# A fused linear-attention and gated-FFN kernel: one list of steps exchanged for another

## The chip, the cores and the metric

The kernel runs on one core of one Trainium2 chip. The metric is the device time of that core in microseconds (us), the median of the runs shown. Five engines work side by side: TensorE (PE in the profile, with PEld for its weight loads), VectorE (DVE), ScalarE (ACT), GpSimd (POOL) and SyncE (SP). Here POOL and SP do almost nothing but issue DMAs. Each engine takes its instructions strictly in program order; semaphores hold an instruction until what it reads has been written.

## The reference

Eight batches, eight heads, 576 positions, head size 64. Per batch and head a 64x64 matrix `kv` is made from k and v, q is multiplied by it, and each row of the product is normalised. The heads are laid side by side (512 columns) and go through a feed-forward part with a gate made by a convolution over three positions.

```python
kv = np.einsum('bhsd,bhse->bhde', k, v)
out = np.einsum('bhsd,bhde->bhse', q, kv)
rms = np.sqrt(np.mean(out * out, axis=-1, keepdims=True) + 1e-06)
attn = out / rms * g_norm                       # -> x: (8, 576, 512)
h = np.maximum(x @ w_in, 0.0)                   # (8, 576, 1024)
for k in range(3):
    conv_out += conv_w[k][None, None, :] * hp[:, k:k + S, :]
gate = 1.0 / (1.0 + np.exp(-conv_out))
result = h * gate @ w_out                       # (8, 576, 512)
```

Inputs and output are 32-bit floats. Inside, the operands of the matrix products are bf16.

## The kernel before

The whole program is unrolled from one string, `ORDER` (line 67). Each word of it is a step: `name.arguments:choice@slots`. A loop (line 802) calls the function of that name; what the function issues goes to the end of the queue of the engine that does it. After the loop every instruction is tied behind the one before it on its engine, so `ORDER` fixes the order on all five engines at once, the order of the DMA issues included. There is no scheduler behind it. The `choice` says which of two engines does a copy or a relu; the `slots` say which PSUM bank (0 to 7) or which buffer of a small ring a step writes, and a step waits until the last readers of that slot are done.

The steps, in the order in which a batch b passes them (t is one of four pairs of heads, f one of eight blocks of 128 columns of h, j a pair of such blocks, e a half of the positions):

- `Lq`, `Lk`, `Lv` (line 304) load q, k or v of a batch from memory, 576 KB in bf16, from POOL's queue; `Li` and `Lo` load a quarter of w_in and a half of w_out the same way. Batch 0 comes in smaller pieces and batch 1 in halves (288 KB). q, k and v have two buffers each (`@0`, `@1`), so a load waits until the batch that was in its buffer has been used.
- `kv.b.0.4` multiplies k by v for all head pairs (line 361, 48 products of one batch). `kvc`, or `kvn` with `ky` or `kx`, copy the result to SBUF: `kvn` straight, `ky` a half of it crossed over by an engine, `kx` the same by a DMA from SP's queue.
- q is transposed: by PE (`qt`, `qtp`) and a copy (`qc`) in batches 0 to 4, by a transposing DMA from SP's queue (`dq.b.0`, `dq.b.1`, line 439) in batches 5, 6 and 7.
- `ot` or `oq` multiplies q by kv, `sq` squares it on ACT, `oc` copies it to SBUF; `on` or `ss` sums the squares on PE, `nl` or `ln` takes the reciprocal root on ACT; `mu0` or `mu` multiplies into x on DVE. From batch 2 on the factors are spread over the positions by PE (`sl`, `sp`), for batches 6 and 7 through memory (`fw`, `fr`).
- `hm.b.f` is the product x times w_in (line 643), for the first blocks split into `ha` and `hb`; `re` is the relu, on ACT (line 649) or DVE (line 651).
- `ta`, `aa`, `ab` make the convolution on DVE, `sg` the sigmoid on ACT, `mg` the product with h on DVE. Sigmoid and reciprocal root need different tables, so ACT reloads a table at each change.
- `om.p.m` is the product with w_out for 128 positions of a pair p of batches (line 764), in one go or in two halves; `ea` copies it out of PSUM, `st` stores it from SP's queue. The last tile is split (`oh`, `eh`, `sh`).
- `unread` issues matrix products that nobody reads; `pl` fills a small mask on POOL; `al` takes a buffer for x or h.

The batches are taken in the order 0, 1, 2, 3, 4, 5, 7, 6 up to the normalisation. While PE makes h of one batch, DVE and ACT work on the gate of the one before, and loads run one to two batches ahead. In the list before, the loads of the last two batches stand in this order, with their buffers:

```python
Lq.7.0@0 Lv.7.0@0 Lk.7.0@0 Lv.6.0@1 Lk.6.0@1 Lq.6.0@1
```

Of the kernel before, what the change touches and what calls it, by code (L numbers as in the profile page):

```python
# [67 lines left out]
pre@0,0,0 Lq.1.0@1 unread.10.0@1 qt0.0.0@0 qt0.0.1@1 ca.k.0:1 pi ca.v.0:1 qc0.0.0:1@0 unread.2.2@2  # L68
kv.0.0.1@3 pn kv.0.1.1@2 kvc.0.0.1.0:1@0 kvc.0.0.1.1 kvc.0.1.1.1 qc0.0.1 unread.3.4@0 kvc.0.1.1.0 ot.0.1@4 ct@1
unread.1.3@0 sq.0.1@0 pg Li.1 unread.2.1@2 on.0.1@0 ot.0.0@6 qt0.0.2@2 pc Li.3 nl.0.1@0 Lk.1.0@1 sq.0.0@0 al.x0@0  # L70
kv.0.2.1@3 kvc.0.2.1.0:1 kvc.0.2.1.1:1 unread.1.1@0 Lv.1.0@1 Li.0 mu0.0.1 on.0.0@0 qc0.0.2:1@0 nl.0.0@1 Lk.1.2 al.h0@0
qt0.0.3@3 ot.0.2@4 sq.0.2@0 kv.0.3.1@2,0 mu0.0.0 qc0.0.3:1 on.0.2@6 unread.3.2@1 kvc.0.3.1.0 kvc.0.3.1.1:1 nl.0.2@0
# [15 lines left out]
qc.4.0:1@0 hm.2.4@0 om.0.2.4 re.2.4 sg.1.6 sg.1.1 sp.3.1@6,3 sg.1.0 ea.0.0:1@2 mu.3.1.1 mu.3.1.0 Lq.5.0@1 hm.2.2@0
aa.1.2 kv.4.0.4@5 re.2.2 ea.0.2@3 Lv.5.0@1 kvn.4.0.4 sp.3.0@6,3 mu.3.0.1 hm.2.5@0 sg.1.3 mu.3.0.0 ab.1.2 hm.2.7@2
re.2.5 dq.5.0@2 re.2.7 hm.3.5@6 mg.1.0 mg.1.3 hm.3.4@0 ky.4.0.4.0 Lk.5.0@1 sg.1.2 hm.2.6@2 ky.4.0.4.1:1 oq.4.0@4  # L90
re.3.4:1 oq.4.1@0 sg.1.5 ta.2.4@0 re.3.5 dq.5.1@1 re.2.6 ta.2.5 sq.4.0@0 oc.4.0@0 hm.3.1@6 re.3.1 mg.1.1 hm.3.3@2
aa.2.2 qtp.4.1@4 sq.4.1@1 qc.4.1@0 hm.3.6@6 oc.4.1 sg.1.4 mg.1.2 om.0.8.0@0 oq.4.2@4 re.3.3 oq.4.3@2 Lq.7.0@0 re.3.6
# [758 lines left out]
```

## Time and profile before

| what | us |
|---|---|
| time, median of three runs | 176.12 (176.03 to 178.52) |
| span of the profiled execution, first to last instruction | 174.7 |
| PE busy | 164.6 |
| DVE busy | 151.8 |
| ACT busy | 144.0 |
| POOL busy | 30.8 |

The profile is of one execution; it gives its span, and the time of that execution beyond the span is not given with it. Between the span and the median of the three runs lie 1.4 us.

Besides the page, four kinds of answers of the trace are used below. A table by windows gives for each stretch of the span its length and, per engine, the busy time and the number of instructions, then PE's granted clock, the DMA share and the bytes moved. A timeline row is start, duration, engine, line, operation, out<-in, shape and count, with the idle time before it in brackets and what ended it; a `q` behind the engine's name means its sequencer, which issues a DMA. A group row has busy time and mean duration of one behind the bar. A DMA row is out<-in, the issuing queue, count, KB, and the us from issue to landing.

### The profile page before, as it was taken

To read this page: it belongs to the slowest core of one execution; us is meant where nothing else is said; L and a number is where in the kernel's file an instruction comes from. 1 tells how busy PE (TensorE), PEld (TensorE's weight loads), DVE (VectorE), ACT (ScalarE), POOL (GpSimd) and SP (SyncE) were. 2 spreads that over 40 slices of the span, in tenths; PEclk is the share of its full clock that TensorE was granted. 3 is DMA by queue.
4 is the path that set the end of the run, shared out by engine and by line. 5 is a ranking of instruction groups with operands and counts; after the bars stand their busy time and mean duration, and the time that the engine had idled before them with its cause. 6 is when DMAs were issued, how large, how long until landed. Compare 5 with 4: busy or idle time off the path is not lost.

```text
span 174.7 us, 3978 instructions
## 1 busy us (share of the span) xinstructions
PE 164.6 (94%) x1590; PEld 100.1 (57%) x1607; DVE 151.8 (87%) x248; ACT 144.0 (82%) x224; POOL 30.8 (18%) x54
## 2 busy tenths in 40 slices
PE   6988997899799999999999999999999999999992
PEld 2545765685644687744677774545687654444451
DVE  4166799999999999999999999999989999998520
ACT  4578897999999999999999998999988629766132
POOL 7994705313130001810000000000000000000000
PEclk9999999999999999999999999999999999999999
DMA  5999999999999999999999390477694400076285
GB/s 151 182 186 198 200 202 203 205 204 204 208 203 205 203 204 164 162 196 191 190 203 234 72 261 6 149 188 181 173 268 161 152 0 4 23 277 235 90 322 196
DMA packets 37450, 30.81 MB, mean 176 GB/s; under 512 B 8608, under 2 KB 32952, under 8 KB 37432
## 3 DMA queue, kind: packets, MB, share of 16 engines
q0 software_dynamic: 21760, 15.96, 60.7%
q1 hardware_dynamic: 15632, 14.59, 29.6%
q8 instruction: 12, 0.20, 0.4%
q14 instruction: 6, 0.05, 0.1%
q10 hardware_dynamic: 40, 0.01, 0.0%
HBM read 34.88 MB, written 9.73 MB: 255 GB/s over the span
## 4 chain that ended last, share of the span: by engine, by line
PE 76%; DVE 9%; DMA 4%; POOL 4%; ACT 2%; issue 2%; POOLq 0%; ACTq 0%
PE bank L764 35%; PE bank L643 30%; DMA w_in_sb<-in_moe_w_in_dram 4%; PE bank L361 3%; PE bank L467 2%; DVE taps L703 1%; DVE qT L346 1%; POOL q_sb L245 1%; DVE taps L709 1%; DVE h L754 1%; PE bank L606 1%; DVE taps L702 1%; POOL v_sb L245 1%; POOL k_sb L245 1%; PE bank L781 1%
## 5 line engine op out<-in xcount | busy, mean ns | idle before, releaser
L643 PE MATMUL bank<-xT,w_in_sb 128*128 128x288 bf16 x480 | 63.6, 286 | 0.3 <-ACT root L545 0.2
L764 PE MATMUL bank<-w_out_sb,h 128*128 128x512 bf16 x267 | 62.4, 379 | 0.8 <-issue 0.3
L643 PEld LDWEIGHTS <-w_in_sb 128*128 128x128 bf16 x480 | 46.0, 98 | 14.9 <-issue 1.6
L748 ACT ACTIVATE taps<-taps,cwn 128x1152 bf16<-128x1152 bf16 (+1 forms) x38 | 39.7, 1078 | 7.4 <-DVE taps L715 7.3
L764 PEld LDWEIGHTS <-h 128*128 128x128 bf16 x280 | 26.4, 98 | 31.0 <-issue 1.2
L649 ACT ACTIVATE h<-bank 128x576 bf16<-128x576 f32 x48 | 30.2, 656 | 3.0 <-PE bank L643 2.8
L344 ACT ACTIVATE row<-bank 128x512 f32<-128x512 f32 (+1 forms) x29 | 16.3, 595 | 8.8 <-PE bank L764 6.0
L754 DVE TENSOR_TENSOR h<-h,taps 128x2304 bf16<-128x2304 bf16 (+1 forms) x20 | 22.0, 1109 | 0.6 <-ACT taps L748 0.6
L709 DVE TENSOR_TENSOR taps<-taps 128x2304 bf16<-128x2304 bf16 (+1 forms) x19 | 21.5, 1134 | 0.2
L715 DVE TENSOR_TENSOR taps<-taps,h 128x2304 bf16<-128x2304 bf16 (+1 forms) x19 | 21.5, 1131 | 0.2
L496 ACT ACTIVATE sq<-bank 128x576 bf16<-128x576 f32 x28 | 17.8, 663 | 0.6 <-PE bank L467 0.3
L703 DVE TENSOR_SCALAR taps<-h,cwn 128x1152 bf16<-128x1152 bf16 (+1 forms) x38 | 17.8, 467 | 0.0
L702 DVE TENSOR_SCALAR taps<-h,cwn 128x1152 bf16<-128x1152 bf16 (+1 forms) x38 | 17.4, 457 | 0.3 <-ACT h L649 0.2
L217 ACT ACT_TABLE_LOAD x12 | 15.4, 1283 | 2.6 <-issue 2.4
L651 DVE TENSOR_SCALAR h<-bank 128x576 bf16<-128x576 f32 x16 | 11.8, 752 | 1.7 <-PE bank L643 0.8
L344 ACT ACTIVATE o<-bank 128x576 f32<-128x576 f32 x19 | 12.8, 674 | 0.0
L632 DVE SCALAR_TENSOR_TENSOR xT<-o,cw,bank 128x576 bf16<-128x576 f32 x16 | 12.2, 808 | 0.1
L304 POOL DMA_DIRECT2D q_sb<-in_q_dram x8 | 6.2, 770 | 30.2 <-PE bank L391 29.4
L430 PE MATMUL bank<-fill 128*128 128x512 bf16 x25 | 9.0, 481 | 1.5 <-DVE fill L232 1.5
L346 DVE COPY row<-bank 128x512 f32<-128x512 f32 (+1 forms) x8 | 5.4, 672 | 4.4 <-PE bank L781 2.4
L361 PE MATMUL bank<-v_sb,k_sb 96*64 96x64 bf16 x384 | 8.3, 197 | 0.7 <-ACT sq L496 0.5
L361 PEld LDWEIGHTS <-k_sb 96*64 96x64 bf16 x384 | 7.1, 112 | 2.9 <-issue 2.2
(94 smaller groups left out, 148.8 us busy)
## 6 DMA issues: line engine op xcount, KB each, us to landing
out_dram<-row SPq DMA_DIRECT2D x35, 256.0 KB, 2.6
q_sb<-in_q_dram POOLq DMA_DIRECT2D x6, 576.0 KB, 15.2
v_sb<-in_v_dram POOLq DMA_DIRECT2D x6, 576.0 KB, 14.6
k_sb<-in_k_dram POOLq DMA_DIRECT2D x6, 576.0 KB, 16.6
factor<-factor SPq DMA_DIRECT2D x8, 288.0 KB, 5.4
w_in_sb<-in_moe_w_in_dram POOLq DMA_DIRECT2D x4, 256.0 KB, 9.0
w_out_sb<-in_moe_w_out_dram POOLq DMA_DIRECT2D x2, 512.0 KB, 18.3
q_sb<-in_q_dram POOLq DMA_DIRECT2D x4, 144.0 KB, 4.7
```

Of the source, the lines that this page charges most:

```text
L344: nc.scalar.activation(to, fr, AX.Copy)
L361: nc.tensor.matmul(ps[i][i * D:(i + 1) * D, t - t0, :], k_sb[:, 2 * t + i, r * D:(r + 1) * D], v_sb[:, 2 * t + i, r * D:(r + 1) * D], star ...
L496: nc.scalar.activation(in_order(b, s), product(b, t), AX.Square)
L643: nc.tensor.matmul(ps[:, e, :HS], w_in_sb[:, t, f * P:(f + 1) * P], x[:, t, e * HS:(e + 1) * HS], start=(t == 0), stop=(t == NT - 1))
L649: nc.scalar.activation(to, fr, AX.Relu)
L702: nc.vector.tensor_scalar_mul(tap[:, 0, f % 2, :n, 8:8 + S], h[:, f], cwn[:, 0, f:f + 1])
L703: nc.vector.tensor_scalar_mul(tap[:, 1, f % 2, :n, :S], h[:, f], cwn[:, 2, f:f + 1])
L709: nc.vector.tensor_add(tap[:, 1, :, :n, :S], tap[:, 0, :, :n, 7:7 + S], tap[:, 1, :, :n, 1:1 + S])
L715: nc.vector.tensor_add(y, y, h[:, 2 * j:2 * j + 2])
L748: nc.scalar.activation(y, y, AX.Sigmoid, scale=cwn[:, 1, f:f + 1])
L754: nc.vector.tensor_mul(h, h, T["tap", c, j][:, 1, :, :n, :S])
L764: nc.tensor.matmul(T["om", p, m], h[:, f, m * P:(m + 1) * P], w_out_sb[:, f, :], start=(f == 0), stop=(f == NF - 1))
```

## The change

`ORDER` is replaced as a whole by another list of the same length. The set of steps is the same: the same products, copies, loads and stores, and 12 table loads in both. Engine by engine the order is the same up to the last head pair of batch 0; from the step `ha` on the lists part ways. Then:

- On PE the steps of one stage change places with each other; the stages follow each other as before.
- Relus: 53 on ACT and 11 on DVE, where it was 48 and 16. Copies `ea` of the output: 24 on ACT and 11 on DVE, where it was 28 and 7. `kvn`: all six on ACT, where it was four. `ky`: 3 on ACT and 5 on DVE, where it was 5 and 3. `kvc.1.2.2` (two copies) and `dg.7` (three) go from ACT to DVE.
- POOL: the loads of batch 3 stand as `Lk Lv Lq`, where it was `Lv Lk Lq`; of batch 5 as `Lq Lk Lv`, where it was `Lq Lv Lk`; `pl` moves behind `Lo.0`. The loads of the last two batches become `Lq.7@0 Lv.7@0 Lk.6@0 Lk.7@1 Lq.6@1 Lv.6@1`.
- SP: `dq.5.1 dq.5.0 st.0.2 st.0.1 st.0.3 dq.7.0 dq.7.1 kx.7 ...`, where it was `dq.5.0 dq.5.1 st.0.0 dq.7.0 kx.7 ...` with `dq.7.1` behind two stores after `kx.7`.
- The buffers for `kvn` are taken ahead of the loop, because a `ky` may now stand ahead of its `kvn`.

The core of the diff, first the stretch of batches 1 to 3, then the loads of the last batches and what stands around `kv.7`, then the function:

```diff
 ORDER = """
...
-sq.1.1@0 kvc.1.2.2.1 on.1.1@4 qc.1.1@0 kvc.1.2.2.0 ot.1.3@2 mg.0.3 Li.2 ta.0.1 ot.1.2@0 nl.1.1@0 mu0.1.1 hm.0.4@4
-sq.1.2@0 sq.1.3@1 Lq.2.0@0 re.0.4 pl on.1.2@6 Lv.2.0@0 aa.0.0 on.1.3@4 nl.1.2@0 ab.0.0 mu0.1.2 nl.1.3@1 hm.0.5@6
-qtp.2.0@0 mu0.1.3 re.0.5:1 ha.1.2@4 sg.0.1 hb.1.2 qc.2.0@0 ta.0.4@0 hm.1.6@2 sg.0.3 qtp.2.1@0 Lk.2.0@0 ta.0.5 aa.0.2
-sg.0.0 hm.1.1@6 ab.0.2 re.1.2 qc.2.1@1 sg.0.2 ha.1.3@4 ta.1.2@3 re.1.1 sg.0.4 sg.0.5 hb.1.3 mg.0.0 re.1.6 hm.1.7@6
-al.h1@1 kv.2.0.4@0 re.1.7 mg.0.1 re.1.3 kvn.2.0.4:1 ky.2.0.4.1 hm.1.0@2 hm.1.5@6 ky.2.0.4.0 re.1.0 ta.1.6@1 re.1.5
-oq.2.0@0 oq.2.1@4 sq.2.0@0 sq.2.1@1 hm.1.4@2 mg.0.2 ta.1.7 ta.1.3 ta.1.0@0 oq.2.2@6 Lv.3.0@1 oc.2.0:1@0 aa.1.3 oc.2.1
-oq.2.3@0 Lk.3.0@1 aa.1.1 Lq.3.0@1 kv.3.0.4@4 ta.1.1 sq.2.2@2 sq.2.3@3 ss.2@5 kvn.3.0.4:1 re.1.4 oc.2.2:1@1 qtp.3.0@2
-Lo.0 oc.2.3 ky.3.0.4.1 ky.3.0.4.0 ln.8@0 qtp.3.1@0 qc.3.0@0 qc.3.1@1 oq.3.1@6 oq.3.0@2 ab.1.3 oq.3.2@0 sq.3.0@0
...
-Lv.7.0@0 kv.5.0.4@1 sq.4.2@2 oc.4.2@1 ab.2.2 hm.2.3@6 ta.2.6@2 kvn.5.0.4 sq.4.3@3 hm.3.7@4 oc.4.3 ky.5.0.4.0:1
-Lk.7.0@0 hm.3.2@2 ky.5.0.4.1:1 sg.2.5 sg.2.4 re.3.7:1 oq.5.0@4 om.0.8.4 sq.5.0@4 om.0.6.0@1 re.2.3:1 oq.5.1@6 re.3.2:1
-oc.5.0@2 oq.5.2@2 ea.0.8@4 oq.5.3@4 sq.5.2@5 om.0.4.0@0 oc.5.2@3 om.0.6.4 Lv.6.0@1 mg.2.2 ta.2.7 aa.2.3 om.0.4.4
...
-oc.5.3 st.0.0 ta.2.3 sl.2@0 re.2.1 Lk.6.0@1 ea.0.5@2 aa.2.1 sp.4.0@4,6 mu.4.0.1 om.0.7.0@2 re.2.0 kv.7.0.4@3
-sp.4.1@0,6 om.0.7.4 mu.4.0.0 hm.3.0@4 dq.7.0@3 sg.2.7 mu.4.1.1 mu.4.1.0 hm.4.6@6 al.h2@0 sg.2.6 re.3.0 ea.0.7@7
...
+re.0.1 mu0.1.0 ot.1.1@4 sq.1.1@0 kv.1.2.2@6 qc.1.1@0 Lk.3.0@1 on.1.1@0 kvc.1.2.2.1:1 unread.3.1@7 kvc.1.2.2.0:1
+nl.1.1@1 ta.0.1 Lv.3.0@1 ot.1.2@2 ot.1.3@6 mu0.1.1 sq.1.2@5 hm.0.4@0 Lq.3.0@1 sq.1.3@0 aa.0.0 Lo.0 on.1.2@4 re.0.4
+ab.0.0 pl nl.1.2@1 on.1.3@0 ta.0.4@3 nl.1.3@0 hm.0.5@4 mu0.1.2 mu0.1.3 hm.1.1@2 Lo.1 mg.0.3 sg.0.1 hm.1.6@6 re.0.5:1
+re.1.1 ha.1.2@0 sg.0.3 ta.0.5 hb.1.2 sg.0.2 aa.0.2 qtp.2.1@4 sg.0.0 ab.0.2 hm.1.7@2 re.1.6 qc.2.1@0 re.1.2 qtp.2.0@6
+ta.1.6@0 sg.0.4 kv.2.0.4@4 Lq.4.0@0 qc.2.0@2 sg.0.5 hm.1.5@0 mg.0.1 Lv.4.0@0 ky.2.0.4.1 re.1.7 ta.1.2@2 Lk.4.0@0
+ha.1.3@6 kvn.2.0.4 ky.2.0.4.0 ta.1.7 re.1.5 oq.2.1@4 oq.2.0@2 aa.1.3 hb.1.3 sq.2.0@0 hm.1.4@0 re.1.3:1 oc.2.0@0 mg.0.2
+sq.2.1@7 hm.1.0@6 re.1.4 mg.0.0 oc.2.1 oq.2.2@0 al.x2@0 ab.1.3 kv.3.0.4@2 re.1.0 ta.1.3 sq.2.2@5 oq.2.3@4 ky.3.0.4.1:1
+sq.2.3@2 ta.1.0@1 kvn.3.0.4 ss.2@6 oc.2.2@2 ky.3.0.4.0:1 ta.1.4@3 oc.2.3 qtp.3.0@2 ta.1.5 qtp.3.1@4 qc.3.0@1 Lq.5.0@1
+qc.3.1@2 ln.8@0 oq.3.1@2 oq.3.0@0 Lk.5.0@1 sq.3.1@0 aa.1.1 oq.3.2@5 om.0.2.0@7 sq.3.0@2 Lv.5.0@1 ab.1.1 sq.3.2@3
...
+re.3.1 oc.4.1 aa.2.2 qtp.4.1@0 sg.1.5 hm.3.6@4 Lq.7.0@0 re.3.3 qc.4.1@2 Lv.7.0@0 om.0.8.0@3 sg.1.4 ab.2.2 Lk.6.0@0
+re.3.6 oq.4.3@6 oq.4.2@0 kv.5.0.4@2 sq.4.3@3 mg.1.2 sq.4.2@5 hm.3.7@4 Lk.7.0@1 ky.5.0.4.1:1 sg.2.5 oc.4.2:1@3 Lq.6.0@1
+om.0.8.4 re.3.7:1 kvn.5.0.4 Lv.6.0@1 sg.2.4 hm.2.3@0 ky.5.0.4.0:1 oc.4.3:1 ea.0.8@1 ta.2.6@2 oq.5.1@4 oq.5.0@6
+om.0.6.0@2 re.2.3 dq.7.0@0 ta.2.7 sq.5.0@7 hm.3.2@0 sq.5.1@4 mg.2.2 oc.5.0@2 om.0.4.0@3 dq.7.1@2 re.3.2 aa.2.3 oc.5.1
...
+hm.2.1@0 ea.0.4@0 sl.2@0 oc.5.3 om.0.5.4 re.2.1 ea.0.6@2 hm.2.0@6 ea.0.5@7 aa.2.1 sp.4.0@0,2 re.2.0 om.0.7.0@4
+mu.4.0.1 kv.7.0.4@5 mu.4.0.0 sp.4.1@2,6 sg.2.7 om.0.7.4 mu.4.1.0 mu.4.1.1 hm.3.0@0 kvn.7.0.4 al.h2@0 sg.2.6 kx.7.0.4.1
...
 """
...
+    for b in QUAD:
+        T["kvn", b] = consts.tile([P, NT, D], BF16, name=f"kvn{b}")
+        T["kvx", b] = consts.tile([P, NT, D], BF16, name=f"kvx{b}")
+
     @op
     def kvn(b, t0, n):
-        if t0 == 0:
-            T["kvn", b] = consts.tile([P, NT, D], BF16, name=f"kvn{b}")
-            T["kvx", b] = consts.tile([P, NT, D], BF16, name=f"kvx{b}")
         copy(T["kvn", b][:, t0:t0 + n], T["kvps", b, t0][0], pick[0] == 0)
```

More of the change, by code (lines that the diff above doesn't have):

```diff
@@ L67 @@
 ORDER = """
[L68 to L72, printed above, removed]
@@ L88 @@
[L88 to L92, printed above, removed]
@@ L118 @@
-ea.3.4:1@1 ea.3.0@0 om.3.6.4 st.2.0 om.3.5.4 om.3.3.4 om.3.2.4 st.3.4 st.3.0 ea.3.6:1@2 ea.3.5:1@3 oh.3.8.0@5 st.3.6
-om.3.1.4 eh.3.8.0:1@4 st.2.5 ea.3.2@1 st.3.5 st.3.2 ea.3.3@2 st.3.3 om.3.7.4 ea.3.1@0 unread.1.2@0 sh.3.8.0 ea.3.7@0
-st.3.1 st.3.7 oh.3.8.1 eh.3.8.1 sh.3.8.1
+pre@0,0,0 al.x0@0 al.h1@1 al.x1@1 unread.10.0@1 pi pn ca.k.0:1 ca.v.0:1 al.h0@0 qt0.0.0@0 qc0.0.0:1@0 qt0.0.1@1
+unread.2.2@2 kv.0.0.1@3 kvc.0.0.1.0:1@0 qc0.0.1 kv.0.1.1@2 kvc.0.0.1.1 unread.3.4@0 Lq.1.0@1 kvc.0.1.1.1 kvc.0.1.1.0
@@ new lines @@
+ot.0.1@4 Li.1 ct@1 unread.1.3@0 sq.0.1@0 pg unread.2.1@2 pc Li.3 on.0.1@0 ot.0.0@6 nl.0.1@0 Lk.1.0@1 qt0.0.2@2
+kv.0.2.1@3 sq.0.0@0 Lv.1.0@1 unread.1.1@0 kvc.0.2.1.0:1 qc0.0.2:1@0 kvc.0.2.1.1:1 on.0.0@0 mu0.0.1 Li.0 qt0.0.3@3
+nl.0.0@1 ot.0.2@4 Lk.1.2 kv.0.3.1@2,0 mu0.0.0 sq.0.2@0 Lq.1.2 qc0.0.3:1 kvc.0.3.1.1:1 on.0.2@6 unread.3.2@1
+kvc.0.3.1.0 nl.0.2@0 Lv.1.2 ot.0.3@2 qt.1.0@0 mu0.0.2 sqh.0.3.0@0 sqh.0.3.1 onh.0.3.0@6 qc.1.0@0 onh.0.3.1 nlh.0.3.0@1
+Li.2 ha.0.3@4 nlh.0.3.1 muh.0.3.0 dg.6 ha.0.2@0 muh.0.3.1 dg.7:1 Lq.2.0@0 hb.0.3 hb.0.2 re.0.3 ps hm.0.6@2 re.0.2:1
@@ new lines @@
+qc.3.1@2 ln.8@0 oq.3.1@2 oq.3.0@0 Lk.5.0@1 sq.3.1@0 aa.1.1 oq.3.2@5 om.0.2.0@7 sq.3.0@2 Lv.5.0@1 ab.1.1 sq.3.2@3
+om.0.1.0@4 oc.3.0@1 ta.1.1 oc.3.1 sl.8@0 om.0.3.0@0 oc.3.2@3 oq.3.3@2 om.0.1.4 sq.3.3@5 aa.1.0 oc.3.3 om.0.3.4 ab.1.0
+ea.0.1@7 sp.2.0@2,5 ea.0.3@0 ss.3@1 mu.2.0.0 om.0.0.0@4 ln.1@0 mu.2.0.1 sp.2.1@0,2 om.0.0.4 mu.2.1.0 sg.1.1 qtp.4.0@5
+mu.2.1.1 hm.2.4@0 qc.4.0:1@2 sl.1@0 om.0.2.4 ea.0.0@3 re.2.4 sp.3.1@4,2 sg.1.2 hm.2.2@0 mu.3.1.0 sg.1.0 mu.3.1.1
+kv.4.0.4@4 re.2.2 aa.1.2 sg.1.7 sp.3.0@2,0 hm.2.5@5 mu.3.0.1 kvn.4.0.4 sg.1.6 mu.3.0.0 hm.2.7@0 ky.4.0.4.0 re.2.5
@@ L121 @@
+unread.1.2@0 sh.3.8.0 eh.3.8.1:1 sh.3.8.1
 """
```

53 lines of the change are left out of this document (26 added, 27 removed).

## The prediction

> **What bounds the kernel now.** I read the page first, for the engine that is full.
>
> ```profile
> span 174.7 us, 3978 instructions
> PE 164.6 (94%) x1590; PEld 100.1 (57%) x1607; DVE 151.8 (87%) x248; ACT 144.0 (82%) x224; POOL 30.8 (18%) x54
> PE   6988997899799999999999999999999999999992
> ```
>
> PE is busy in 164.6 of 174.7 us, and its row of tenths is full from the twelfth slice to the last but one. No reordering changes the amount of PE work, so all that can be won are PE's idle 10.1 us, and whatever makes PE wait anew is lost. Where these 10.1 us lie is in the table by windows (stretch, length, then busy us of PE, PEld, DVE, ACT, POOL, PE's clock, DMA share, GB/s):
>
> ```profile
> 26.00:31.60 5.60, 3.88 (x66) 2.52 (x67) 5.26 (x10) 4.67 (x11) 3.52 (x5) 1.00 1.33 203
> 40.00:48.00 8.00, 6.64 (x126) 4.68 (x124) 8.00 (x20) 7.87 (x15) 2.28 (x4) 1.00 1.28 207
> 48.00:86.00 38.00, 37.55 (x403) 22.27 (x409) 37.32 (x63) 37.45 (x63) 6.39 (x8) 1.00 1.27 191
> 86.00:168.00 82.00, 81.53 (x617) 48.25 (x617) 76.61 (x98) 64.62 (x88) 0.00 (x0) 1.00 0.56 153
> 168.00:174.70 6.70, 3.27 (x22) 1.77 (x21) 0.56 (x1) 2.23 (x5) 0.00 (x0) 0.96 0.67 245
> ```
>
> PE idles 1.72 us in 26 to 31.6, 1.36 in 40 to 48, then 0.45 in 38 us and 0.47 in 82 us; the 3.4 us at the end are the last copy, the last store and the program's end. From 48 on PE alone sets the end. Before 48 the chain of waits runs through DVE:
>
> ```profile
> 46.63 0.31 DVE qT L346
> 46.94 0.35 issue
> 47.29 0.75 DVE qT L346
> 48.04 0.04 issue
> 48.09 0.32 PE bank L467 x4
> ```
>
> The two copies `qc.3.0` and `qc.3.1` release the products `oq.3`, and DVE had no idle time in 40 to 48. A third resource is hidden behind both: the loads. In the same windows GB/s stands at 191 to 207; POOL's queue delivers at a steady pace, in issue order, and several loads land just ahead of their use.
>
> **Part 1: the stage up to 48 us.** What the first products with w_out allow is bounded from below by a load:
>
> ```profile
> 30.40 1.52 POOL L325 DMA_DIRECT2D w_out_sb<-in_moe_w_out_dram  x2
> w_out_sb<-in_moe_w_out_dram POOLq DMA_DIRECT2D x1, 512.0 KB, 17.4
> 48.40 0.32 PE bank L764
> ```
>
> The first half of w_out is issued at 30.40 and lands 17.4 us later, at 47.8; the first of these products runs at 48.4. The new list issues the same bytes ahead of it (k, v and q of batch 3 only change places), so it lands at 47.8 again: at most **0.6 us** can be won here. What can be lost is read from DVE's steps between `mu0.1.0`, which waits for the same ACT chain in both lists, and `qc.3.1`. The groups (busy us and mean ns behind the bar):
>
> ```profile
> L651 DVE TENSOR_SCALAR h<-bank 128x576 bf16<-128x576 f32 x16 | 11.8, 752 | 1.7 <-PE bank L643 0.8 <-PE bank L666 0.7
> L346 DVE COPY o<-bank 128x576 f32<-128x576 f32 x5 | 3.7, 749 | 0.0
> L346 DVE CAST kvx<-bank 64x256 bf16<-64x256 f32 x3 | 1.3, 420 | 0.1
> L346 DVE CAST kvn<-bank 128x256 bf16<-128x256 f32 x2 | 0.8, 414 | 0.0
> L346 DVE CAST kvbd<-bank 64x64 bf16<-64x64 f32 x4 | 0.9, 222 | 4.5 <-PE bank L361 4.5
> L703 DVE TENSOR_SCALAR taps<-h,cwn 128x576 bf16<-128x576 bf16 x14 | 5.5, 389 | 0.0
> L702 DVE TENSOR_SCALAR taps<-h,cwn 128x576 bf16<-128x576 bf16 x14 | 5.1, 361 | 0.1
> ```
>
> Into this stretch come the two copies `kvc.1.2.2`, a shape that DVE does not have before (between the 222 ns of the smaller cast and the 414 of the larger; I take 0.3 each, as it is nearer in size to the smaller), `re.1.3` (0.75), two `ky.3` (2 x 0.42) and `ta.1.4`, `ta.1.5` (2 x 0.75): 3.7 us. Out go `kvn.2`, `kvn.3` (2 x 0.41), `oc.2.0`, `oc.2.2` (2 x 0.75) and `ta.1.1` (0.75): 3.1. An add comes (`ab.1.3`) and one of the same shape goes (`aa.1.1`). That is **+0.6** in front of `qc.3.1`. Against it stands that the three copies of `dg.7` and one relu less lie before `mu0.1.0`, where DVE waits for ACT anyway. I take +0.5. Worse is possible: `hm.1.1` now follows `hm.0.5` directly and needs `mu0.1.3`, where the old list had a transpose and `ha.1.2` as cover; a wait of the length of those two (20 products) costs nothing if PE still waits for `qc.3.0` later, and some 0.8 more if DVE is pushed back by it. So this part is +0.5, between -0.6 and +1.3. PE has no slack after 48 to take it back.
>
> **Part 2: the loads of batches 7 and 6.** `kv.7` needs k and v of batch 7. In the old list k of batch 7 is the third load of the last six, in the new one the fourth, behind k of batch 6. The rows of POOL, and the landings of q, v, k (batch 7), v and, two further on, q (batch 6):
>
> ```profile
> 69.11 0.77 POOL L304 DMA_DIRECT2D q_sb<-in_q_dram  x1 [19.53 <-PE bank L391]
> 69.87 0.77 POOL L304 DMA_DIRECT2D v_sb<-in_v_dram  x1
> 70.63 0.77 POOL L304 DMA_DIRECT2D k_sb<-in_k_dram  x1
> 72.19 1.10 POOL L304 DMA_DIRECT2D v_sb<-in_v_dram  x1 [0.80 <-PE bank L361]
> ...
> 74.04 0.77 POOL L304 DMA_DIRECT2D q_sb<-in_q_dram  x1
> ```
>
> ```profile
> q_sb<-in_q_dram POOLq DMA_DIRECT2D x1, 576.0 KB, 8.0
> v_sb<-in_v_dram POOLq DMA_DIRECT2D x1, 576.0 KB, 10.2
> k_sb<-in_k_dram POOLq DMA_DIRECT2D x1, 576.0 KB, 13.5
> v_sb<-in_v_dram POOLq DMA_DIRECT2D x1, 576.0 KB, 16.1
> q_sb<-in_q_dram POOLq DMA_DIRECT2D x1, 576.0 KB, 19.5
> ```
>
> Issue plus landing time gives 77.1, 80.1, 84.1, 88.3 and 93.5: first, second, third, fourth and sixth. All are 576 KB and land in issue order, so the place decides. The first is not held by the stream but by POOL, which stood until PE's transpose `qtp.4.1` had freed the buffer; that step has the same PE work ahead of it in both lists, so the clock of the six starts at the same place. PE wants them here:
>
> ```profile
> 85.73 0.95 PE L361 MATMUL bank<-v_sb,k_sb 96*64 96x64 bf16 x48
> 94.27 0.95 PE L361 MATMUL bank<-v_sb,k_sb 96*64 96x64 bf16 x48
> ```
>
> `kv.7` starts at 85.73, 1.6 us after its k landed; the PE work ahead of it is the same in both lists. With k landing fourth it starts at 88.3: **+2.6 us**, on PE, with nothing behind it that could go ahead. A delay from part 1 moves both sides alike, since the transpose moves with PE. `kv.6` needs v of batch 6, now sixth: 93.5 against 94.27 + 2.6; a spare of 3.4 us, no wait.
>
> How firm is the 88.3? The stream has two paces there: 3.0 us from first to second, then 4.0 and 4.2. What slows it is the transposing DMA of q:
>
> ```profile
> 77.15 2.20 SPq L439 DMA_TRANSPOSE qT<-q_sb  x1
> qT<-q_sb SPq DMA_TRANSPOSE x1, 11.6
> ```
>
> It is issued when q of batch 7 has landed and lands itself at 88.8. Without it, four loads at 3.0 would put k at 77.1 + 9.0 = 86.1, a wait of 0.4 us. The new list issues `dq.7.0` at the same event, and `dq.7.1` right behind it. If the second took a toll of its own in the same stretch (88.3 - 86.1 = 2.2), k would land at 90.5, a wait of 4.8. I take 2.6, since the one transpose is what the rows show and it alone fills the time to 88.8; ends +0.4 and +4.8.
>
> [...]
>
> The rest of the queues: on SP three stores of pair 0 now stand ahead of `dq.7.0` where one stood; they need tiles that were copied out long before and fall between 69 and 72, before the first load's data. On ACT `kvn.7` now stands ahead of `sg.2.6` and two more steps, and ACT will stand at it until `kv.7` is done; DVE stands at `mu.4.1`, for the spread products behind `kv.7`. Both go on as late as PE does, and ACT has 17 us of idle time after 86.
>
> **Part 3: after 92 us.** The order of `hm`, `om` and the copies changes, five relus fewer and four output copies more are on DVE. By the window 86 to 168 DVE has 5.4 us to spare and ACT 17.4; PE has 0.47 to give back. I take -0.2 (between -0.4 and +0.5, if a relu or copy comes late for a bank). The end is the same chain, product, copy, store: 0.
>
> **Sum.** +0.5 + 2.6 - 0.2 = +2.9 us on the span: 177.6. The median of the runs lies 1.4 above the span of the profiled execution; so **179.0 us**, 1.6% slower. About 2%, 3.5 us, is what a measurement of this kernel can tell from no change, and this stays inside it.
>
> **The rivals.**
>
> *The second transpose takes its toll before k of batch 7.* Place: the stream between 80 and 90. For it: the two transposes are queued together. Against it: the first alone lasted 11.6 us, to the very time at which the fourth load lands. Price 2.2 us more: 176.1 + 0.5 + 4.8 - 0.2 = 181.2, slower by 2.9%. It crosses 2% once k lands after 88.9.
>
> *k comes in time.* If the transposes' packets come later against the loads than before, the stream keeps its 3.0 us: 176.1 + 0.5 + 0.4 - 0.2 = 176.8, and 175.7 with part 1 at its lower bound: no change. For it: the transposes need not start at the same moment. Against it: `dq.7.0` waits for the same landing as before. It decides where k lands before 86.
>
> *The first stage costs more.* DVE and the missing cover before `hm.1.1`: +1.3 in place of +0.5, and as much again if batches 2 and 3 (their `mu`, `sp`) are late for `hm.2`: 180 to 181. For it: DVE is full from 31.6 to 48. Against it: over the whole way to `mu.2.0.0` as much leaves DVE (`re.0.3`, two `kvn`, two `oc`: 3.1 us) as comes (`re.1.3`, two `ky`, two `kvc`: 2.2, and the three copies of `dg.7`, at 0.2 to 0.4 each by the casts above), so only the order inside can cost.
>
> That the list isn't carried out as written is no case: each engine's order is fixed.
>
> **How the numbers follow.** The forecast has 0.58, the toll 0.17, k in time 0.14, the first stage 0.11. From 176.5 to 181.6 lie all of the forecast, the toll, most of the third and part of the second; some 0.15 is outside. Slower by over 2% (above 179.6): the toll, two thirds of the first stage, and the forecast's upper edge (0.07): 0.31. Faster by over 2% would need 3.5 of the 4.0 us that PE idles between 26 and 168: 0.01. The rest, 0.68, is within 2%.
>
> **What will show it.** In the profile after, `kv.7` should have an idle time of 2 to 3 us before it, ended by the DMA of k, at about 86 to 89 us; DVE and ACT should have idle times beside it; PE should be full from there to 168. The first product with w_out should stand at 48.5 to 49.5. If k of batch 7 lands less than 17 us after the issue of the first load (before, the fourth took 88.3 - 69.1 = 19.2) or PE has no idle time before `kv.7`, part 2 is wrong; if PE waits for something else after 92, part 3.

## The result and the profile after

The new list takes 182.63 us (median of four runs, 182.0 to 184.36), the old one beside it 176.53 (176.03 to 178.52): 1.0346 times as long, interval 1.0264 to 1.0428. Forecast were 179.0 and a range that ended at 181.6. The profiled execution is one of 182.0 us with a span of 180.2, which is 5.5 more than before; forecast were 2.9. Single executions of one kernel differ by 0.6 to 4.6 us here, and a good part of that goes with the mean clock that PE was granted (0.98 to 1.00), so where it matters that clock stands beside the span. All four executions of the new kernel had a mean clock of 0.987 to 0.991; the profiled one is the fastest of them, so its 5.5 us fall 0.6 short of the 6.1 between the medians.

The page after, first the engines, then the rows of tenths:

```profile
span 180.2 us, 3981 instructions
PE 166.4 (92%) x1590; PEld 100.3 (56%) x1607; DVE 153.5 (85%) x253; ACT 144.3 (80%) x219; POOL 30.7 (17%) x54
PE   6788998999699999999799999999999999999992
PEclk9999999999969999999999999999999999999999
```

Two rows answer different questions. PE's row has two dents, in the eleventh slice and in the twentieth; there PE waited. The row of the clock has a 6 in the twelfth, where PE's own row has a 9: PE looks busy there and gets less done. The table by windows (stretch, length, busy us of PE, PEld, DVE, ACT, POOL, clock, DMA share, GB/s) puts numbers to it:

```profile
26.00:31.60 5.60, 4.65 (x58) 2.71 (x54) 5.33 (x12) 4.80 (x9) 3.83 (x8) 1.00 1.33 204
40.00:48.00 8.00, 6.66 (x119) 4.70 (x117) 7.77 (x19) 7.93 (x16) 0.54 (x1) 1.00 1.28 206
48.00:49.00 1.00, 0.30 (x8) 0.23 (x9) 1.00 (x2) 0.99 (x2) 0.73 (x1) 0.98 1.25 205
49.00:52.00 3.00, 2.61 (x16) 1.02 (x10) 2.93 (x7) 2.92 (x7) 1.58 (x3) 0.50 1.30 202
52.00:53.00 1.00, 1.00 (x6) 0.37 (x5) 0.93 (x4) 0.47 (x1) 0.00 (x0) 0.82 1.32 205
53.00:86.00 33.00, 32.61 (x358) 19.67 (x361) 30.24 (x47) 31.43 (x51) 4.62 (x6) 1.00 1.19 195
86.00:92.00 6.00, 4.40 (x74) 2.54 (x74) 4.04 (x7) 5.47 (x9) 0.00 (x0) 1.00 1.28 191
92.00:168.00 76.00, 75.12 (x543) 44.95 (x548) 73.19 (x93) 61.62 (x83) 0.00 (x0) 1.00 0.53 138
```

PE idles 1.60 us between 86 and 92, where a wait of 2.6 was forecast, and behind that only 0.88 in 76 us. Not forecast: from 48.96 to 52.36 its clock is 0.50. Before, the clock was 1.00 in every one of these stretches. The chain of waits shows what that does to the first products with w_out (line 764 before, 765 after). After:

```profile
40.32 0.39 ACT kvx L344
...
40.75 0.44 PE bank L468 x8
...
44.02 0.88 PE bank L361 x48
...
45.18 0.42 DVE kvx L346
...
47.88 0.15 DVE qT L346
48.03 0.52 issue
48.56 0.76 DVE qT L346
...
50.57 3.21 PE bank L765 x10
```

Before, the same chain:

```profile
45.35 0.36 DVE taps L703
45.71 0.33 DVE kvn L346
46.04 0.36 DVE o L346
46.40 0.23 issue
...
48.78 2.32 PE bank L764 x10
```

The copies `qc.3.0` and `qc.3.1` (qT) start 1.25 and 1.27 later (47.88 and 48.56 against 46.63 and 47.29), and ten products take 3.21 us in place of 2.32. A second thing is to be read in this chain: before, DVE's own row, one piece behind the other, was the chain up to `qc.3.0`; now it comes over ACT, whose copy `ky.2` (kvx) ends at 40.71 and releases `oq.2.1`, then over PE, which ends `kv.3` at 44.90, and only then over DVE, which works off `ky.3` (kvx) and three taps.

Now the loads: the timeline of PE at line 361, then of POOL (first, fourth and sixth of the six last loads), then what those three took from issue to landing:

```profile
90.38 0.95 PE L361 MATMUL bank<-v_sb,k_sb 96*64 96x64 bf16 x48 [1.44 <-DMA k_sb<-in_k_dram]
99.48 0.95 PE L361 MATMUL bank<-v_sb,k_sb 96*64 96x64 bf16 x48 [0.45 <-ACT h L650]
```

```profile
71.97 0.77 POOL L304 DMA_DIRECT2D q_sb<-in_q_dram  x1 [21.30 <-PE bank L391]
...
75.05 0.78 POOL L304 DMA_DIRECT2D k_sb<-in_k_dram  x1 [0.78 <-PE bank L361]
...
76.72 0.77 POOL L304 DMA_DIRECT2D v_sb<-in_v_dram  x1
```

```profile
q_sb<-in_q_dram POOLq DMA_DIRECT2D x1, 576.0 KB, 6.1
k_sb<-in_k_dram POOLq DMA_DIRECT2D x1, 576.0 KB, 15.3
v_sb<-in_v_dram POOLq DMA_DIRECT2D x1, 576.0 KB, 22.6
```

`kv.7` waits 1.44 us for k of batch 7, which lands at 75.05 + 15.3 = 90.3. `kv.6` waits 0.45 us. The row names a relu on ACT, but that relu (`re.4.4`) is not in `kv.6`'s bank, and the one that is (`re.4.5`) was done at 98.57; v of batch 6 lands at 76.72 + 22.6 = 99.3. It was the load.

Set side by side, the starts of a few steps on PE tell where the 5.5 us come from:

| step | before | after | later by | forecast |
|---|---|---|---|---|
| `oq.3.1`, behind the copies of the first stage | 47.42 | 48.70 | 1.28 | 0.5 |
| `sp.2.0`, behind the first w_out products | 53.11 | 55.80 | 2.69 | 0.5 |
| `sp.4.0` | 84.53 | 87.66 | 3.13 | 0.5 |
| `kv.7` | 85.73 | 90.38 | 4.65 | 3.1 |
| `kv.6` | 94.27 | 99.48 | 5.21 | 3.1 |
| span | 174.7 | 180.2 | 5.5 | 2.9 |

So: 1.3 by the copies, 1.4 by the clock, 0.4 in small steps, 1.5 at `kv.7`, 0.6 at `kv.6`, 0.3 behind it. The experiments ask whether these terms are what they look like.

### The profile page after: what moved, and what is told of

The parts are those of the page before. It is cut to its first block, busy times and chain, and to the rows that moved or that the text cites. A ratio compares the mean times of both kernels' runs of the same rounds, so it can differ in the third digit from the quotient of the medians.

```text
span 180.2 us, 3981 instructions
## 1 busy us (share of the span) xinstructions
PE 166.4 (92%) x1590; PEld 100.3 (56%) x1607; DVE 153.5 (85%) x253; ACT 144.3 (80%) x219; POOL 30.7 (17%) x54
## 4 chain that ended last, share of the span: by engine, by line
PE 63%; DMA 14%; ACT 10%; issue 4%; POOL 4%; DVE 3%; SPq 0%; DVEq 0%; POOLq 0%
PE bank L765 28%; PE bank L644 26%; DMA k_sb<-in_k_dram 8%; DMA w_in_sb<-in_moe_w_in_dram 4%; PE bank L361 3%; ACT h L650 3%; PE bank L468 2%; ACT taps L749 2%; POOL q_sb L245 1%; DMA out_dram<-row 1%; ACT L217 1%; ACT root L546 1%; POOL v_sb L245 1%; POOL k_sb L245 1%; PE bank L659 1%
## 5 line engine op out<-in xcount | busy, mean ns | idle before, releaser
L765 PE MATMUL bank<-w_out_sb,h 128*128 128x512 bf16 x267 | 63.7, 384 | 0.9 <-issue 0.4
L765 PEld LDWEIGHTS <-h 128*128 128x128 bf16 x280 | 26.9, 99 | 31.6 <-issue 3.1
L650 ACT ACTIVATE h<-bank 128x576 bf16<-128x576 f32 x53 | 33.6, 654 | 5.7 <-PE bank L644 4.8
L344 ACT ACTIVATE row<-bank 128x512 f32<-128x512 f32 x24 | 14.0, 597 | 11.1 <-PE bank L765 11.0
L497 ACT ACTIVATE sq<-bank 128x576 bf16<-128x576 f32 x28 | 17.4, 656 | 2.9 <-PE bank L468 2.5
L217 ACT ACT_TABLE_LOAD x12 | 15.4, 1283 | 2.6 <-issue 2.4
L704 DVE TENSOR_SCALAR taps<-h,cwn 128x1152 bf16<-128x1152 bf16 (+1 forms) x38 | 17.4, 459 | 0.0
L346 DVE COPY row<-bank 128x512 f32<-128x512 f32 (+2 forms) x13 | 8.2, 647 | 5.2 <-PE bank L765 4.5
L344 ACT ACTIVATE o<-bank 128x576 f32<-128x576 f32 x19 | 12.1, 662 | 0.0
L430 PE MATMUL bank<-fill 128*128 128x512 bf16 x25 | 8.4, 453 | 1.6 <-DVE fill L232 1.5
L652 DVE TENSOR_SCALAR h<-bank 128x576 bf16<-128x576 f32 x11 | 8.2, 753 | 1.5 <-PE bank L644 1.4
## 6 DMA issues: line engine op xcount, KB each, us to landing
v_sb<-in_v_dram POOLq DMA_DIRECT2D x6, 576.0 KB, 15.4
k_sb<-in_k_dram POOLq DMA_DIRECT2D x6, 576.0 KB, 15.4
```

The source lines that it names most:

```text
L344: nc.scalar.activation(to, fr, AX.Copy)
L497: nc.scalar.activation(in_order(b, s), product(b, t), AX.Square)
L650: nc.scalar.activation(to, fr, AX.Relu)
L704: nc.vector.tensor_scalar_mul(tap[:, 1, f % 2, :n, :S], h[:, f], cwn[:, 2, f:f + 1])
L765: nc.tensor.matmul(T["om", p, m], h[:, f, m * P:(m + 1) * P], w_out_sb[:, f, :], start=(f == 0), stop=(f == NF - 1))
```

## The experiments

Where starts of different runs are compared, they are counted from `hm.0.5` (31.61 before, 31.37 after), since the first 31 us of single executions differ by some tenths, in three of them by 1 to 3 us.

### The loads put back, and the loads moved alone

First the new kernel with only the six loads in the old order:

```diff
-Lq.7.0@0 ... Lv.7.0@0 ... Lk.6.0@0 ... Lk.7.0@1 ... Lq.6.0@1 ... Lv.6.0@1
+Lq.7.0@0 ... Lv.7.0@0 ... Lk.7.0@0 ... Lv.6.0@1 ... Lk.6.0@1 ... Lq.6.0@1
```

> The new kernel, with only the six last loads put back into the old order (q, v, k of batch 7, then v, k, q of batch 6); the two transposes of q of batch 7 stay behind each other. My theory, place in the stream: all loads still land 4.0 to 4.2 us apart, but k of batch 7 is third again and lands at about 86.2 us, ahead of PE, which gets there at 88.9; kv.7 has no idle time before it, kv.6 has none either (v of batch 6 fourth, at 90.3), and the span falls from 180.2 by 1.4 + 0.5 to about 178.2 us. Rival, the wait only moves: q of batch 6 is sixth and lands at about 99, its transposes come late for oq.6, and the span stays at 179.7 or more.

Measured: 180.23 us, 1.0185 [1.0134, 1.0237] times the old kernel; span of the profile 178.2. Its timeline of PE (lines 361 and 468):

```profile
87.63 0.95 PE L361 MATMUL bank<-v_sb,k_sb 96*64 96x64 bf16 x48
96.21 0.95 PE L361 MATMUL bank<-v_sb,k_sb 96*64 96x64 bf16 x48
...
97.84 0.31 PE L468 MATMUL bank<-qT,kvx 64*64 64x288 bf16 x1 [0.45 <-DMA kvx<-kvn]
```

Both waits for loads are gone. The span is the forecast one by accident: in this execution the clock stayed at 1.00, which alone is worth 1.3 us, and a wait appeared that no theory had: in `oq.7.0` PE idles 0.64 us for the copies `kx.7`, and 1.50 us pass from its start (97.09) to the next step, where the old kernel needs 0.25. These are SP's DMAs, issued behind the second transpose at 90.05 and 90.65, and landed at 97.8 and 98.3, some 7.7 us later; in the old kernel, where only the first transpose is issued ahead of them, they take 3.0. That the same stage, with the same waits, once lost its clock and once did not (two of this kernel's four executions had 1.000 and spans of 177.0 and 178.2, two had 0.990 and 178.7 and 178.8) was the first hint that the clock isn't decided by the kernel alone.

Then the other way round, the old kernel with only its six loads in the new order:

> The old kernel, with only the six last loads in the new order (k of batch 7 fourth, v of batch 6 sixth); one transpose of q of batch 7 runs beside them, as before. Theory of the place: k lands fourth at about 88.3, kv.7 waits and starts there, 2.6 us later than before; v of batch 6 lands at 93.5, ahead of kv.6: span 177.3. Rival, the second transpose makes the lateness: with one transpose the fourth load lands at 86 to 86.5 and the span is 174.9 to 175.4.

Three of its four executions had mean clocks of 0.979 to 0.981, and the profiled one among them (span 179.9) lost its clock twice, from 7.6 to 11 and from 89.6 to 93 us; the fourth (0.998) had a span of 176.6. The times are 178.42 to 183.06 us. In the profile `kv.7` waits as the theory of the place said, k landing at 89.2, 11.1 us behind q, as the fourth load did before (88.3 - 77.1 = 11.2). The timeline of PE, and the windows of 3.41 us up to the end of that wait and behind it:

```profile
89.23 1.30 PE L361 MATMUL bank<-v_sb,k_sb 96*64 96x64 bf16 x48 [2.40 <-DMA k_sb<-in_k_dram]
```

```profile
86.15:89.56 3.41, 1.00 (x24) 0.42 (x23) 1.96 (x3) 3.38 (x4) 0.00 (x0) 1.00 1.32 195
89.56:92.97 3.41, 3.41 (x50) 1.83 (x44) 2.02 (x3) 0.52 (x1) 0.00 (x0) 0.50 1.21 182
```

PE was busy in 1.00 of 3.41 us, and then had half the clock for 3.41 us; `kv.7` took 1.30 in place of 0.95. A wait has a second price.

### The second transpose alone

The old kernel with `dq.7.1` moved directly behind `dq.7.0`:

```diff
-... dq.7.0@3 ... kx.7.0.4.1 ... kx.7.0.4.0 ... dq.7.1@0
+... dq.7.0@3 dq.7.1@0 ... kx.7.0.4.1 ... kx.7.0.4.0
```

> The old kernel, with only the second transpose of q of batch 7 moved directly behind the first, so that both are queued while the last loads land. Theory, the second takes a toll of its own: the first three or four loads land as before (77.1, 80.1, 84.1, 88.3), or up to 1 us later, the fifth and sixth are slowed too, and q of batch 6 lands at 96 to 98 in place of 93.5; kv.7 keeps its start at 85.7 and the span stays at 174.7 within 0.5 us. Rival, one queue, no second share: q of batch 6 lands at 93.5 as before, the second transpose only after it. If k is slowed past 85.7, the span grows by what it is late.

Measured: 177.8 us, 1.0066 [1.0039, 1.0093]. The six loads (first, fourth and sixth here, issued at 68.72, 71.81 and 73.66) and the row of PE that explains the span of 176.3:

```profile
q_sb<-in_q_dram POOLq DMA_DIRECT2D x1, 576.0 KB, 9.2
v_sb<-in_v_dram POOLq DMA_DIRECT2D x1, 576.0 KB, 17.0
q_sb<-in_q_dram POOLq DMA_DIRECT2D x1, 576.0 KB, 24.8
```

```profile
95.96 0.75 PE L467 MATMUL bank<-qT,kvx 64*64 64x288 bf16 x2 [0.89 <-DMA kvx<-kvn]
```

The first four land as before (77.9 to 88.8), the sixth at 98.5 in place of 93.5. `kv.7` doesn't wait. The loads bear the theory out; the span doesn't, because `oq.7.0` waits for the copies `kx.7`, issued behind the second transpose as in the run above (PE idles 1.03 us in all, and 1.88 us pass to the next step in place of 0.25). From the first landing to the fourth it takes 11.1 to 11.5 us with one transpose (the old kernel, the run with its loads moved, the run that follows) and 10.9 to 12.3 with two (the new kernel, its loads put back, this run, and the filled run below); to the sixth 16.4 to 17.4 with one and 20.5 to 21.3 with two. The toll of the second falls behind the fourth load.

### The new order of the loads with one transpose

The new kernel with `dq.7.1` behind `kx.7` and with the five unread products that the next part explains:

```diff
-... dq.7.0@0 ... dq.7.1@2 ... kx.7.0.4.0
+... dq.7.0@0 ... kx.7.0.4.0 dq.7.1@2
```

> The new kernel with the new order of the six last loads, with the second transpose of q of batch 7 put back behind the two copies of kvx.7, and with the five unread products between 46 and 49 us. PE is at kv.7 by 87.7. With both transposes beside the loads, k of batch 7 landed 12.0 us behind q of batch 7 (77.13 and 89.10), PE waited 1.54 before kv.7, and v of batch 6 landed 20.7 behind. Theory, the place in the stream is most of it and the second transpose little up to the fourth load: k lands 11.1 to 11.3 behind q, PE waits 0.6 to 1.5 before kv.7; v of batch 6 lands 16.5 to 17.5 behind and kv.6 doesn't wait; span 177.8 to 178.5. Rival, the second transpose is what makes k late: k lands 9.5 to 10.2 behind q, no wait, span 177.1 as with the old order of the loads.

Measured: 181.21 us, 1.0265 [1.0209, 1.032], span 179.5. In its timeline:

```profile
90.17 0.95 PE L361 MATMUL bank<-v_sb,k_sb 96*64 96x64 bf16 x48 [0.75 <-DMA k_sb<-in_k_dram]
```

k lands 11.5 behind q, v of batch 6 17.4 behind q, and `kv.6` doesn't wait: the theory of the place, and of the transpose at `kv.6`. The span missed: 177.8 to 178.5 was forecast, and the four executions have 179.0 to 179.8. The same kernel with the old order of the loads is the run that follows:

> The new kernel with the old order of the six last loads, with the second transpose of q of batch 7 put back behind the two copies of kvx.7 on SP, and with the five unread products between 46 and 49 us. Theory: no wait before kv.7, before kv.6 or inside oq.7, no low clock; what is left is the copies' lateness in the first stage: oq.3.1 at 48.7, span 174.7 + 1.4 = 176.1, some 177.6 us. Rival, the order after 92 us costs something by itself that the waits covered until now: span over 177.

Measured: 178.93 us, 1.0118 [1.0057, 1.0179], all four executions with a clock of 0.999 or more and spans of 176.6 to 177.3. None of the three waits is left. Between these two kernels only the order of six loads differs. At full clock the first had spans of 179.3 and 179.8: the order of the loads is worth 2.5 us, more than the 0.75 that the profiled execution shows, which had lost clock at its start (`hm.0.5` at 33.20) and so came to `kv.7` late; no profile shows one of the two at full clock, so what the 2.5 us consist of there is not shown. The span of 177.1 is 1.0 above the forecast for what was left. Counted from `hm.0.5`, `oq.3.1` is 1.5 later than before, `sp.4.0` 2.1, and from there nothing but 0.3 is added: the rival, a cost behind 92 us, is small, and the first stage and the small steps behind it are the rest.

### The clock

In the new kernel the longest idle time of PE between 45 and 49 us is 0.72. Five products of a constant tile, into a free bank that a later step overwrites, fill these gaps without moving what PE waits for:

```diff
-... qtp.3.0@2 ... oq.3.1@2
+... unread.2.0@7 qtp.3.0@2 ... unread.3.0@7 oq.3.1@2
```

> The new kernel, with five products of the constant tile with itself, whose result nobody reads, put where PE idles: two ahead of the first transpose of batch 3's q, three ahead of oq.3.1. Theory, PE's clock fell because PE was too idle between 45 and 49 us: with the idle time filled the granted clock stays at 1.00 from 48 to 53 us, the first ten w_out products take 2.3 us in place of 3.2, and the span falls by 1.2 to 1.4 us, to about 178.9. Rival, the clock falls for another cause (the first w_out products, or the DMA traffic there): it is 0.50 from 49 to 52 again and the span is 180.2 to 180.6.

The windows of the profile, first the old kernel's up to 49 us, then two of this run:

```profile
45.00:49.00 4.00, 3.04 (x51) 2.11 (x49) 4.00 (x9) 3.92 (x8) 1.73 (x3) 1.00 1.24 206
```

```profile
45.00:49.00 4.00, 3.56 (x49) 2.04 (x46) 3.87 (x11) 3.97 (x7) 0.74 (x1) 1.00 1.24 206
49.00:52.00 3.00, 2.77 (x22) 1.20 (x15) 2.93 (x7) 2.92 (x7) 1.57 (x3) 1.00 1.31 204
```

The clock stays at 1.00, `sp.2.0` comes 1.33 us earlier behind `hm.0.5`, and the span is 178.7: the price of the low clock, as forecast. The median, 181.38 us (1.0295 [1.0222, 1.0368]), is less clear, since two of four executions still had 0.987 and 0.991 and some 2 us more (without the products it was all four). The wait before `kv.7` was left, and so it was filled too; if PE's idleness is what costs the clock, hardly an execution should lose it now:

```diff
-... kv.7.0.4@5
+... unread.6.0@5 kv.7.0.4@5
```

> The new kernel with unread products of the constant tile in both places where PE idles: five between 46 and 49 us and six directly ahead of kv.7. The waits themselves stay. [...] Rival, the clock falls whatever PE does there: some executions show 0.987 to 0.991 again, and 182 us or more.

Three of four executions had 1.000, one 0.990. The time is no better for it: 182.24 us, 1.0308 [1.0214, 1.0402]. The profile (clock 1.00, span 180.6) has PE idle for 0.94 us between 98.5 and 100, ahead of `kv.6`, where the new kernel's has 0.45. Filling kept the clock in most executions and doesn't shorten a wait.

The plain test is the old kernel, made to wait. Two taps ahead of `qc.3.0`:

```diff
-... qc.3.0@0 qc.3.1@1 ... ta.1.4@2 ... ta.1.5
+... ta.1.4@2 ta.1.5 qc.3.0@0 qc.3.1@1
```

> The old kernel with the two taps ta.1.4 and ta.1.5 ahead of the copies qc.3.0 and qc.3.1 on DVE. Theory, PE follows DVE here: oq.3.1 comes 1.3 us later, at 48.7, and the span is 176.0, 177.4 us in executions with the clock at 0.997 or more; PE then idles some 2.5 us in 45 to 49, as in the new kernel, so that some executions have 0.990 and are 1.5 us longer still. Rival, DVE's order doesn't matter as its work is the same: sp.2.0 stays at 53.1 and the span at 174.7.

Measured: 178.72 us, 1.0064 [1.0015, 1.0112]; seven of the ten executions had 0.990 or less and two more lay at 174.9 and 175.9 with 1.00, one at 175.7 with 0.996. `oq.3.1` came 1.1 us later behind `hm.0.5`, as the work put ahead of it says. Then the same with seven unread products in the gap of 1.67 us:

```diff
-... oq.3.1@6
+... unread.7.0@4 oq.3.1@6
```

> The old kernel with the two taps ahead of qc.3.0, as in the run with the taps ahead, where 7 of 10 executions had a clock of 0.99 or less, and with seven unread products ahead of oq.3.1, where PE then idles 1.67 us. The wait stays, only PE is busy in it. Theory, the idle PE makes the clock fall: the clock is 0.996 or more in at least 8 of 10 executions and the median is 177.4, the span 175.7 to 176.0 in the profile (1.1 over the old kernel's). Rival, the clock falls for another cause at the first w_out products: 0.99 in 7 of 10 again, median 178.7.

Measured: 178.22 us, 1.0097 [1.006, 1.0134]; two of nine executions at 0.990 or less. The windows, first without the products, then with them:

```profile
45.68:49.09 3.41, 1.51 (x33) 1.20 (x30) 3.41 (x9) 3.02 (x6) 2.21 (x3) 1.00 1.25 204
49.09:52.50 3.41, 3.19 (x12) 1.22 (x10) 3.31 (x8) 3.07 (x6) 0.35 (x1) 0.53 1.31 203
```

```profile
45.68:49.09 3.41, 3.10 (x39) 1.90 (x39) 3.41 (x10) 3.34 (x6) 1.53 (x2) 1.00 1.24 206
49.09:52.50 3.41, 3.23 (x24) 1.34 (x20) 3.30 (x8) 3.03 (x7) 1.02 (x2) 1.00 1.30 202
```

Seven of ten against two of nine, with the wait the same, and the w_out products and the traffic too: it points to PE's idleness as what costs the clock, though so few executions could split like this by chance (some 7 in 100). No time was won: the median fell by 0.5 us and stayed 0.8 above the forecast, but the old kernel beside it was 1.05 faster than beside the first (176.47 against 177.52), so the ratio rose from 1.0064 to 1.0097. The executions at 0.996 or more have spans from 175.6 to 178.3, without the products 174.9 to 175.9, so the clock is not all that scatters, and why is open. Last, the old kernel itself with two products in its gap of 0.54 us:

> The old kernel with two unread products of the constant tile ahead of oq.3.1, where PE idles 0.54 us. Of the executions of the old kernel shown so far beside the others, 5 in 23 had a mean clock of 0.99 and were some 1.6 us longer. Theory, those lost one period of 3.4 us at half clock behind this idle stretch: with it filled nearly none does, the median falls to 176.2 to 176.5 and no execution is above 178. Rival, the loss has another place (the first 16 us, where one run of another kernel lost two periods): as many executions at 0.99 as before, the same times.

One of 12 executions lost clock, 4 of 20 of the old kernel beside them (11 of 54 in all these comparisons). 176.24 us against 176.47, a ratio of 0.9976 [0.9943, 1.0009]: not told apart from the old kernel. It is the only version here whose interval reaches 1.

### The first stage

The new list puts three taps between the first half of `ky.3` and the copies of batch 3's q. Without them there, and with the old loads and one transpose:

```diff
-... ta.1.0@1 ... ta.1.4@3 ... ta.1.5 ... qc.3.0@1 qc.3.1@2
+... qc.3.0@1 qc.3.1@2 ta.1.0@1 ta.1.4@3 ta.1.5
```

> As the run with the old loads and the second transpose put back, without the unread products, but with the three taps ta.1.0, ta.1.4 and ta.1.5 behind the two copies of batch 3's q on DVE. Theory, these taps are what makes the first stage late: ky.3.0 ends 0.7 us earlier, both transposes follow it, and qc.3.0 starts at 46.8 to 46.9 in place of 47.88; oq.3.1 at 47.6 to 47.8, the first w_out product at 48.4 to 48.7, span 174.9 to 175.3, 176.4 to 176.8 us, the same as the old kernel. Rival, DVE has as much to do ahead of sl.8 as before and only moves the lateness there: sp.2.0 stays at 54.5 and the span at 176.1.

Measured: 179.9 us, 1.017 [1.0094, 1.0245], not faster than with the taps left where they were (178.93). The chain of waits says why (the execution shown lost its clock from 8.6 to 15.4 us, so all stands 3 us later):

```profile
47.89 1.19 ACT sq L497 x2
49.08 0.28 ACT kvn L344
49.38 0.44 DVE kvx L346
49.86 0.68 PE bank L391 x12
50.57 0.65 DVE qT L346
```

With the taps gone DVE waits: `ky.3.0` follows `kvn.3`, which now is ACT's, behind two squares; and `qtp.3.0` follows `ky.3.0`, because the new list has it in the bank of `kv.3` (2), where the old one kept them apart (2 and 4). `oq.3.1` comes 0.54 earlier, not 1.0, and the taps are missing ahead of `sl.8`, so that `sp.2.0` is 0.3 later. The rival was right about where the lateness goes; the spans of the other three executions, 177.6 to 178.2, lie above its 176.1 too.

In this stage three DVE steps take 0.85, 0.88 and 0.89 us to the next step, 0.8 more together than in the old list, and beside them POOL issues three loads. A memset on POOL that waits for `aa.1.3` holds these loads back:

```diff
-... Lq.4.0@0 ... Lv.4.0@0 ... Lk.4.0@0 ... aa.1.3
+... aa.1.3 hold Lq.4.0@0 Lv.4.0@0 Lk.4.0@0
```

> As the run with the old loads, the second transpose put back and the five unread products, with one more change: a small memset on POOL that waits for aa.1.3 holds the three loads of batch 4 back, so that POOL issues them from about 41.8 us instead of 38.1 to 40.8. In the new list three DVE steps beside these issues, ta.1.2, ta.1.7 and aa.1.3, take 0.85, 0.88 and 0.89 us to the next step, in the old list, without a load beside them, 0.55, 0.56 and 0.67. Theory, the issue of the loads on POOL lengthens them: they go back to 0.55 to 0.67, qc.3.0 and oq.3.1 come 0.8 us earlier behind hm.0.5 (16.5 us instead of 17.3), and the span falls from 177.1 to 176.3, if batch 4 still lands in time for kv.4. Rival, the lengths belong to the order of these steps and what they read: they stay, and the span stays at 177.1.

Measured: 179.33 us, 1.0138 [1.0082, 1.0194]. The profile's span is 176.3, the theory's number, but by luck: `hm.0.5` stood at 30.96 there against 31.66 in the run with the loads beside the steps, and counted from it `oq.3.1` comes 17.32 us later in both. The timeline of DVE, where 0.36 is the tap and the brackets are waits:

```profile
39.08 0.36 DVE L711 TENSOR_SCALAR taps<-h,cwn 128x576 bf16<-128x576 bf16 x1
39.64 0.37 DVE L710 TENSOR_SCALAR taps<-h,cwn 128x576 bf16<-128x576 bf16 x1 [0.20 <-ACT h L657]
...
41.41 0.76 DVE L659 TENSOR_SCALAR h<-bank 128x576 bf16<-128x576 f32 x1 [0.33 <-PE bank L674]
```

The slow taps (0.69 and 0.60 in the new kernel) are back at 0.36, and nothing is gained: DVE now waits 0.20 for `re.1.7` on ACT and 0.33 for `hb.1.3` on PE, and from `mu0.1.0` to `qc.3.1` it takes 22.36 us, to the hundredth what it took with the loads beside it. `hb.1.3` stands behind `oq.2.1`, which waits 0.47 us for `ky.2.0` on ACT. The slow taps were cover for a wait, so the theory was right about the taps and the rival about the time.

## Why the prediction was wrong

**What bounds it.** PE's row and the idle 10.1 us were the right place to look (the list of them leaves out 2.7 us in the first 26), and PE was nearly full behind 92 us. That PE's busy time is not PE's work was not thought of: with the same instructions it rose from 164.6 to 166.4 us.

**Part 1, +0.5.** Mis-sized, and one term is missing. By the list, counted from one start to the next and with the add, instructions of 3.87 us come ahead of `qc.3.1` and of 3.22 go, +0.65 by the trace against the +0.6 of the sum. But the copies came 1.25 and 1.27 us later, at the upper bound, and from `mu0.1.0` to `qc.3.1` it takes 22.36 us in place of 21.19, 1.17 more. The step that failed is the one that took DVE's row as the only chain of the stage. In the profile DVE idles no more than before there (0.42 against 0.41); that the other 0.5 are a wait on other engines is seen in the run that held the loads back, where the taps were short again and the 22.36 stayed. With `kvn.2` and `kvn.3` on ACT and `ky.3` on DVE the chain runs ACT, PE, DVE at `oq.2.1`, and, with the taps gone, ACT, DVE, PE at `qtp.3.0`. Taking away what looked like the cause (three taps, three slow steps) moved the wait and not the end. The bank that `kv.3` and `qtp.3.0` share was not separated in a run; whether it alone would give the 0.5 back is open.

The missing term is the clock: 1.33 us, shown by the filled run. It isn't in the sum at all. Between 45 and 49 us PE was busy for 3.04 us in the old kernel's profile and for 2.43 in the new one's, and the clock fell behind the second; how little is too little was not measured closer than that.

**Part 2, k of batch 7, +2.6.** The mechanism was right: fourth place, a wait ended by the DMA of k, nothing behind it that could go ahead. At full clock the order of the loads is worth 2.5 us. The profile's wait is smaller, 1.44, by the step "a delay from part 1 moves both sides alike". It doesn't: the first load was issued 2.86 us later than before (71.97 against 69.11) and landed 1.0 later (78.1 against 77.1), as it needed 6.1 us in place of 8.0. What PE lost in the first stage it did not lose again here.

**Part 2, v of batch 6, "no wait".** Failed. v was to land at 93.5 with 3.4 us to spare and landed at 99.3. The rate behind the fourth load was taken from the old trace, where only one transpose runs; with the second the sixth lands 20.5 to 21.3 us behind the first load in place of 16.4 to 17.4. The rival that gave it a toll ahead of k fell: in the old kernel the fourth landed at 88.8 with two transposes queued against 88.3 with one. That the second would cost the loads nothing was the author's estimate, from rows that show one transpose alone; with two queued the sixth landed at 98.5 in place of 93.5. Why the toll comes only behind the fourth is not shown.

**Part 3, -0.2.** +0.3 in the profile, inside what was given. Ahead of it lie 0.4 more between `sp.2.0` and `sp.4.0`, for which the sum had nothing: PE idles 0.31 us there before and 0.39 after, and is busy 31.11 and 31.47 us with 353 products in both. Why is open.

**The sum.** +0.5 + 2.6 - 0.2 became 1.3 (copies) + 1.4 (clock) + 0.4 + 1.5 (k) + 0.6 (v) + 0.3. The rival "the first stage costs more" (180 to 181) had half of the cause, and the toll before k came nearest in time (181.2) by a cause that fell; both stay below 182.63, as does the range, and no case of it had the clock and the load together.

## What to carry to other kernels

Read the clock's row beside PE's row: where PE waits often, even in pieces of 0.36 to 0.72 us as here, price the wait with what 3.4 us at half clock cost too (1.33 us at the first w_out products), and where the wait can't be taken away, unread products in it can keep the clock (two of nine executions lost it, where seven of ten did without), though here they won no time in the old kernel. Where several loads run in one stream, the place of a load decided when it landed here (the fourth 10.9 to 12.3 us behind the first, whichever it was), and a transfer moved ahead slowed the last (98.5 in place of 93.5), so the spare of the last ones has to be worked out anew. Before an engine's row is summed up as the bound of a stage, follow its instructions' operands one step to the other engines: what leaves a full engine can come back as a wait for another.
